# GpSimd's convolved channels: from 32 SBUF-to-SBUF transfers a chunk to 12 by way of device memory, with new orders

## The chip, the cores and the metric

One core of one Trainium2 chip. The metric is the device time of the kernel in microseconds (us). Before the change it is 2811.06 us, the median of 3 runs (2805.05 to 2817.03).

## The reference

The input `x` has 8 sequences of 4096 tokens with 192 channels. Each channel goes through a causal filter of 7 taps; the taps are the softmax of `weight`, one set for each of 8 heads of 24 channels. The result goes through a layer with a rational activation:

```python
h = x @ w_in                                  # [32768, 192] @ [192, 2048]
P = a[0] + a[1]*h + a[2]*h**2 + a[3]*h**3
Q = 1.0 + abs(b[0])*abs(h) + abs(b[1])*h**2
out = (P / (Q + 1e-6)) @ w_out                # [32768, 2048] @ [2048, 192]
```

All inputs and outputs are float32.

## The kernel before, in words

The 32768 tokens are worked in 64 chunks of 512. The 2048 hidden features of a chunk are eight units of 256. For a unit `k` the steps are named by one letter each in the order tables:

- `g1` (`gemm1`, L436): ten matmuls on TensorE, five for each half `a` and `b`, from the convolved tokens into a PSUM tile `hp` of which there are two. The five use the high and low part of the weights (`wh_t`, `wl_t`) and of the tokens: `A` (high part of 128 channels), `L` (its low part) and `B` (high and low part of the other 64 channels). The first matmul of the five already reads `A`, the fourth and fifth read `B`.
- `p`, `A`, `B`, `L`, `Y` on ScalarE (L477, L488, L491, L497, L504), `u` on GpSimd (L481), `v`, `m`, `e`, `g` on VectorE (L485, L508, L512, L516), and `Q`, an accumulating DMA that GpSimd issues (L494). They evaluate P/Q. `v` is the last reader of `hp`.
- `g2` (`gemm2`, L454): the second product, into two PSUM tiles `o0` and `o1`, one for each half of the tokens. `O` (L464, L465) evacuates them and stores the result.

The convolution has two parts. Ninety-six channels are convolved on TensorE for two chunks at a time (`c`, L351), into the same PSUM tiles `o0` and `o1`; ScalarE (`xh`, L375) and VectorE (`xl`, L382) turn this into the high and low part in tile `xh0`, which holds `A` and `L`. These two write all 128 partitions; of every 32 partitions the last 8 are then overwritten. The other 96 channels are convolved on GpSimd (`fir`, steps `f0` to `f8`), which leaves their high and low parts in `fh`, laid out as four token quarters of 32 partitions. `fill` (L411) brings them to the tokens' layout with plain DMAs on SyncE's queue (`move`, L409): sixteen of 32 partitions x 128 tokens into tile `xh1`, which is `B`, and sixteen of 8 partitions x 2 x 128 into the rows of `xh0` that are left. The profile drops the numbers of names, so both tiles read as `xh`. `mv0` is the first sixteen, `mv1` the second; the second sixteen have to come after `xl` of their chunk.

What sets the order: three tables of steps (`START`, `PLAN` once for every two chunks, `END`), which fix the order on TensorE, ScalarE, VectorE and GpSimd. In `g10b.3` the digit behind `g1` is the unit, `b` the half, and the number behind the point says how many chunks back from the newest one. The DMAs on SyncE's queue are not held to the table; they stand in the order that the framework gives them, and each waits there for what it needs, with all behind it waiting too. `POOL_H` and `POOL_L` say for which weight blocks GpSimd makes the high part and the low part at the start; the low parts that GpSimd doesn't make take two matmuls and a copy on VectorE.

Of the kernel before, what the change touches and what calls it, by code (L numbers as in the profile page):

```python
# [50 lines left out]


PLAN = """
g23c.5 g24a.5 g24c.5 g25a.5 v0.4 Y6.5 m6.5 p1.4 e6.5 g6.5 L7.5 A1.4 g12a.4 g12b.4 p2.4 Y7.5 f8.3 mv0.3 u1.4
v1.4 m7.5 Q1.4 e7.5 B2.4 u2.4 g25b.5 g25d.5 g25c.5 g26a.5 g13b.4 g7.5 L0.4 f0.2 A2.4 Q2.4 g13a.4 B3.4 g26b.5
g26d.5 v2.4 Y0.4 p3.4 u3.4 A3.4 L1.4 g26c.5 g27a.5 g27b.5 g27d.5 g27c.5 g14b.4 O0.5 m0.4 e0.4 g0.4 O1.5 Y1.4
g14a.4 B4.4 p4.4 v3.4 c0.3 xh0.3 xh0.2 m1.4 e1.4 f1.2 xl0.3 mv1.3 Q3.4 L2.4 u4.4 g1.4 A4.4 Q4.4 xl0.2 f2.2
v4.4 g15b.4 g15a.4 Y2.4 p5.4 B5.4 u5.4 m2.4 e2.4 f3.2 g2.4 L3.4 g20a.4 g20c.4 g21a.4 g21c.4 ld1.1 A5.4 Q5.4
g16a.4 g16b.4 B6.4 v5.4 g20b.4 g20d.4 Y3.4 g21b.4 g21d.4 p6.4 m3.4 u6.4 A6.4 Q6.4 L4.4 f4.2 f5.2 e3.4 g22a.4
g3.4 v6.4 g17a.4 g17b.4 p7.4 g22b.4 Y4.4 m4.4 e4.4 g4.4 g22c.4 g23a.4 g23c.4 B7.4 L5.4 A7.4 u7.4 v7.4 g10b.3  # L60
g10a.3 g22d.4 g23b.4 g23d.4 g24b.4 B0.3 Y5.4 m5.4 e5.4 Q7.4 g5.4 p0.3 f6.2 L6.4 A0.3 u0.3 v0.3 Q0.3 f7.2
ld0.1 g11a.3 g11b.3 p1.3 Y6.4 m6.4 e6.4 g6.4 g24a.4 B1.3 g24c.4 f8.2 mv1.2 mv0.2 g24d.4 u1.3 g25a.4 A1.3
v1.3 g12b.3 g12a.3 L7.4 Q1.3 g25b.4 p2.3 g25d.4 Y7.4 B2.3 A2.3 m7.4 f0.1 L0.3 u2.3 e7.4 Q2.3 g26b.4 g7.4
g26d.4 v2.3 g13b.3 g13a.3 p3.3 Y0.3 m0.3 B3.3 g25c.4 g26a.4 u3.3 L1.3 e0.3 g0.3 g27b.4 A3.3 v3.3 g27d.4 O1.4
g14b.3 g14a.3 Q3.3 p4.3 Y1.3 f1.1 g26c.4 g27a.4 B4.3 L2.3 u4.3 A4.3 Q4.3 m1.3 g20b.3 e1.3 g1.3 g27c.4 f2.1
O0.4 v4.3 g15a.3 g15b.3 B5.3 g20d.3 g20a.3 Y2.3 m2.3 e2.3 p5.3 g2.3 L3.3 g21b.3 g21d.3 A5.3 u5.3 Q5.3 v5.3
g16a.3 g16b.3 B6.3 g20c.3 g21a.3 Y3.3 m3.3 e3.3 f3.1 p6.3 g3.3 A6.3 u6.3 v6.3 L4.3 g22b.3 g22d.3 g17a.3
g17b.3 p7.3 Y4.3 B7.3 g21c.3 g22a.3 g22c.3 f4.1 m4.3 Q6.3 g23a.3 f5.1 e4.3 A7.3 L5.3 g4.3 g10b.2 u7.3 v7.3
ld1.0 g10a.2 p0.2 Y5.3 g23b.3 g23d.3 m5.3 e5.3 Q7.3 B0.2 f6.1 g24b.3 g24d.3 L6.3 f7.1 g11b.2 u0.2 A0.2
g11a.2 B1.2 Q0.2 g5.3  # L70
"""


START = """
wiw0.0 tp1.0 tp0.0 tp8.0 tp9.0 tp2.0 wiw1.0 tp3.0 tp5.0 wia0.0 tp4.0 wis0.0 wio0.0 wid0.0 wid1.0 wia1.0
wir0.0 wih0.0 wiw2.0 ld0.0 wid2.0 tp6.0 c0.0 wis1.0 cf0.0 wio1.0 cf1.0 wia2.0 wis2.0 wio2.0 wir1.0 cf2.0
wil0.0 wih1.0 wow0.0 woa0.0 wir2.0 wih2.0 wos0.0 xh0.0 wod0.0 xh1.0 xl0.0 wil2.0 wip1.0 woo0.0 wor0.0 wiw3.0
wia3.0 wid3.0 wow1.0 xl1.0 wod1.0 wis3.0 wio3.0 wir3.0 wih3.0 cf3.0 woa1.0 wos1.0 wiw4.0 g10a.0 woo1.0 cf4.0
g10b.0 B0.0 wor1.0 p0.0 u0.0 wia4.0 wil1.0 g11a.0 wid4.0 A0.0 Q0.0 wow2.0 wod2.0 wis4.0 wio4.0 wir4.0 woa2.0
wos2.0 woo2.0 wor2.0 v0.0 g11b.0 A1.0 B1.0 Q1.0 wiw5.0 wia5.0 wis5.0 p1.0 wio5.0 u1.0 wih4.0 wip3.0 wil3.0  # L80
g12a.0 wow3.0 ld1.2 wod3.0 woa3.0 wos3.0 wid5.0 wir5.0 woo3.0 wor3.0 v1.0 wip4.0 wih5.0 wil4.0 L0.0 wiw6.0
wia6.0 wid6.0 Y0.0 g12b.0 B2.0 wis6.0 wio6.0 p2.0 wow4.0 woa4.0 m0.0 wod4.0 e0.0 g13a.0 wir6.0 wos4.0 g13b.0
u2.0 wip5.0 ld0.2 B3.0 A2.0 p3.0 woo4.0 wor4.0 wil5.0 v2.0 wiw7.0 wia7.0 wis7.0 wio7.0 g15a.0 Q2.0 g0.0 u3.0
A3.0 wih6.0 wow5.0 wid7.0 woa5.0 wos5.0 wip6.0 wil6.0 L1.0 woo5.0 wir7.0 wod5.0 wor5.0 Y1.0 v3.0 m1.0 Q3.0
g15b.0 p5.0 e1.0 B5.0 ld0.1 c0.1 xh1.1 xl1.1 xh0.1 xl0.1 L2.0 g14a.0 g14b.0 A4.0 f0.2 g20a.0 g20c.0 g1.0
g21a.0 wow6.0 woa6.0 wos6.0 woo6.0 A5.0 Y2.0 g21c.0 u5.0 v5.0 m2.0 e2.0 g2.0 f1.2 f2.2 wow7.0 g16a.0 woa7.0
wos7.0 woo7.0 g16b.0 B4.0 Q4.0 g22a.0 p4.0 u4.0 v4.0 wih7.0 wil7.0 Q5.0 p6.0 L3.0 B6.0 u6.0 g20b.0 g20d.0
f3.2 f4.2 f5.2 g17a.0 ld1.3 Y3.0 wod7.0 m3.0 e3.0 g3.0 A6.0 g17b.0 p7.0 Q6.0 L4.0 Y4.0 g21b.0 g21d.0 wor7.0
g22b.0 g22d.0 g23b.0 B7.0 u7.0 v6.0 A7.0 Q7.0 L5.0 g10b.1 g10a.1 p0.1 f6.2 f7.2 g22c.0 g23a.0 m4.0 e4.0 g4.0
g23d.0 g24b.0 g24d.0 v7.0 Y5.0 g11a.1 m5.0 B0.1 u0.1 e5.0 g5.0 L6.0 wod6.0 A0.1 Q0.1 g11b.1 wor6.0 B1.1  # L90
"""


END = """
Y6.4 f8.2 mv0.2 g23c.4 v0.3 p1.3 m6.4 g24a.4 g24c.4 u1.3 A1.3 g25a.4 f0.1 L7.4 e6.4 g6.4 g12a.3 g12b.3 Q1.3
v1.3 p2.3 Y7.4 m7.4 e7.4 B2.3 u2.3 g7.4 f1.1 A2.3 v2.3 g25b.4 g25d.4 g26b.4 g26d.4 Q2.3 L0.3 g13b.3 g13a.3
p3.3 Y0.3 m0.3 B3.3 u3.3 g25c.4 g26a.4 L1.3 g26c.4 g27b.4 g27d.4 e0.3 O1.4 g0.3 A3.3 f2.1 v3.3 g27a.4 g27c.4
O0.4 g14b.3 g14a.3 Y1.3 Q3.3 c0.2 p4.3 m1.3 B4.3 u4.3 xh0.2 e1.3 xl0.2 mv1.2 g1.3 g15a.3 L2.3 A4.3 v4.3
xh0.1 xl0.1 Y2.3 m2.3 e2.3 g2.3 f3.1 f4.1 Q4.3 g15b.3 B5.3 p5.3 u5.3 g20a.3 A5.3 g20c.3 f5.1 g21a.3 g21c.3
Q5.3 L3.3 g16a.3 g16b.3 B6.3 v5.3 Y3.3 m3.3 e3.3 g3.3 g20b.3 g20d.3 p6.3 u6.3 A6.3 Q6.3 v6.3 L4.3 g22a.3  # L100
g22c.3 f6.1 f7.1 g17b.3 g17a.3 p7.3 Y4.3 m4.3 e4.3 g4.3 B7.3 g21b.3 g21d.3 g22b.3 g23a.3 A7.3 L5.3 g10a.2
g10b.2 p0.2 g22d.3 u7.3 Y5.3 v7.3 B0.2 m5.3 e5.3 g5.3 g23b.3 Q7.3 L6.3 A0.2 u0.2 v0.2 g11b.2 g11a.2 B1.2
Q0.2 Y6.3 m6.3 e6.3 f8.1 mv0.1 mv1.1 p1.2 g6.3 g23c.3 g24a.3 g24c.3 g25a.3 L7.3 A1.2 g12b.2 u1.2 v1.2 Q1.2
g12a.2 p2.2 Y7.3 B2.2 u2.2 m7.3 e7.3 g7.3 L0.2 A2.2 v2.2 g23d.3 g24b.3 g24d.3 Q2.2 g13b.2 g13a.2 p3.2 g25c.3
g25b.3 g25d.3 g26b.3 Y0.2 g14b.2 m0.2 e0.2 B3.2 u3.2 g0.2 L1.2 A3.2 v3.2 g14a.2 p4.2 Y1.2 m1.2 Q3.2 e1.2
g26d.3 g1.2 B4.2 u4.2 g27b.3 g27d.3 L2.2 g15b.2 A4.2 O1.3 Q4.2 g15a.2 p5.2 v4.2 Y2.2 m2.2 e2.2 B5.2 g26a.3
g26c.3 g27a.3 g27c.3 u5.2 g2.2 L3.2 A5.2 g16b.2 Q5.2 g16a.2 B6.2 v5.2 g20b.2 g20d.2 g21b.2 Y3.2 g21d.2 p6.2
L4.2 m3.2 e3.2 g3.2 A6.2 g17a.2 u6.2 Q6.2 g17b.2 O0.3 B7.2 Y4.2 v6.2 m4.2 e4.2 p7.2 A7.2 g22b.2 g4.2 g22d.2
g20a.2 g20c.2 g10b.1 g10a.1 u7.2 L5.2 g21a.2 v7.2 p0.1 Q7.2 Y5.2 m5.2 e5.2 g23b.2 g23d.2 B0.1 g24b.2 g11a.1
u0.1 A0.1 g11b.1 g21c.2 L6.2 g5.2 g22a.2 g22c.2 p1.1 Y6.2 v0.1 m6.2 e6.2 B1.1 A1.1 g6.2 g23a.2 Q0.1 u1.1  # L110
v1.1 Q1.1 g12a.1 L7.2 g12b.1 p2.1 Y7.2 g23c.2 g24a.2 g24c.2 m7.2 e7.2 g7.2 B2.1 u2.1 A2.1 v2.1 Q2.1 L0.1
g13b.1 g13a.1 p3.1 Y0.1 m0.1 e0.1 g0.1 B3.1 u3.1 A3.1 Q3.1 g25a.2 g25c.2 g24d.2 g25b.2 g14b.1 v3.1 L1.1
g14a.1 B4.1 Y1.1 m1.1 e1.1 g1.1 g26a.2 g26c.2 g27a.2 g27c.2 p4.1 u4.1 O0.2 g15b.1 g15a.1 A4.1 v4.1 g25d.2
g26b.2 g26d.2 L2.1 p5.1 Y2.1 m2.1 Q4.1 e2.1 g2.1 B5.1 u5.1 A5.1 v5.1 Q5.1 g16a.1 L3.1 g16b.1 B6.1 g20a.1
g20c.1 g21a.1 Y3.1 p6.1 m3.1 e3.1 g3.1 g17b.1 g17a.1 A6.1 u6.1 v6.1 g21c.1 g22a.1 g22c.1 L4.1 p7.1 Y4.1 m4.1
e4.1 g4.1 g27b.2 g27d.2 B7.1 O1.2 g23a.1 Q6.1 u7.1 g23c.1 A7.1 v7.1 g20b.1 g20d.1 g21b.1 g21d.1 g22b.1 L5.1
Y5.1 g24a.1 g22d.1 g23b.1 L6.1 Y6.1 g23d.1 g24b.1 m5.1 e5.1 m6.1 g5.1 e6.1 Q7.1 g6.1 L7.1 Y7.1 m7.1 g24d.1
e7.1 g25b.1 g24c.1 g25a.1 g25c.1 g26a.1 g26c.1 g25d.1 g26b.1 g26d.1 g7.1 g27a.1 g27c.1 O0.1 g27b.1 g27d.1
O1.1
"""  # L120


# [519 lines left out]
```

## Time and profile before

| what | value |
|---|---|
| median of 3 runs | 2811.06 us |
| the profiled execution's own time | 2802.48 us |
| its span, first to last instruction | 2800.6 us |
| TensorE matmul busy | 2647.5 us, 95% |
| VectorE busy | 2544.2 us, 91% |
| ScalarE busy | 2528.5 us, 90% |
| GpSimd busy | 2291.8 us, 82% |
| mean busy share of the DMA engines in slices | 0.6 to 0.7 |
| mean granted TensorE clock | 0.978 |

The kernel is periodic: two chunks take about 86 us, and the 64 chunks are 32 such pairs, of which 31 have GpSimd's part (the first pair's tokens are convolved on TensorE alone). A busy TensorE is not TensorE at its peak, since matmuls overlap; what it waits for and how long is read from the idle time ahead of an instruction. A wait is put down to what came last by the profile, so that the same wait can carry different names in different pairs.

### The profile page before, as it was taken

What the parts mean: (1) busy time and instruction counts of PE and PEld (TensorE: products, weight loads), DVE (VectorE), ACT (ScalarE), POOL (GpSimd) and SP (SyncE); (2) the same over time, 40 slices, a digit from 0 to 9 for tenths busy, and PEclk for the clock granted to TensorE, in tenths of its full rate; (3) what the DMA queues carried; (4) which work ended last, traced back from release to release, by engine and by line L of the source; (5) the groups of instructions that cost most, each with busy time, mean ns of one, the idle gap of its engine ahead of it and who ended that gap; (6) DMA issues with size and microseconds to landing.
All of it is one profiled execution on the core that took longest, in us unless ns stands there. A gap on an engine that the chain in (4) does not pass through costs nothing.

```text
span 2800.6 us, 50009 instructions
## 1 busy us (share of the span) xinstructions
PE 2647.5 (95%) x18007; PEld 2381.5 (85%) x18007; DVE 2544.2 (91%) x2185; ACT 2528.5 (90%) x2798; POOL 2291.8 (82%) x1866
## 2 busy tenths in 40 slices
...
GB/s 211 129 148 152 128 148 124 147 154 126 144 134 142 157 137 135 139 133 147 154 127 148 130 142 156 132 141 132 138 152 137 138 137 137 147 153 125 139 122 105
DMA packets 207159, 393.81 MB, mean 141 GB/s; under 512 B 37184, under 2 KB 127808, under 8 KB 206912
## 3 DMA queue, kind: packets, MB, share of 16 engines
...
q8 instruction: 142, 2.33, 0.3%
...
q10 hardware_dynamic: 288, 0.04, 0.0%
...
## 4 chain that ended last, share of the span: by engine, by line
PE 45%; SPq 17%; ACT 13%; issue 9%; POOL 6%; DMA 6%; DVE 5%; POOLq 0%; ACTq 0%; DVEq 0%
PE hp L436 23%; PE o L454 21%; SPq L409 17%; ACT t L477 3%; POOL t L481 3%; ACT B L491 3%; ACT B L497 3%; ACT A L488 2%; DMA out<-ob 2%; DMA xh<-fh 2%; DVE y L512 2%; ACT y L504 1%; POOL prod L400 1%; DMA A<-B 1%; POOL A L494 1%
## 5 line engine op out<-in xcount | busy, mean ns | idle before, releaser
L481 POOL TENSOR_TENSOR t<-t,B 128x1024 f32<-128x1024 f32 x512 | 1255.3, 2452 | 432.6 <-ACT t L477 288.9
L454 PE MATMUL o<-wo_t,t 128*128 128x192 f32 x8192 | 1419.2, 328 | 2.3 <-DVE t L516 1.2
L454 PEld LDWEIGHTS o<-wo_t,t 128*128 128x128 f32 x8192 | 1364.0, 191 | 47.8 <-DVE t L516 2.5
L436 PE MATMUL hp<-xh,wh_t 128*128 128x512 f32 x3072 | 1136.8, 424 | 129.7 <-DMA xh<-fh 84.6
L508 DVE SCALAR_TENSOR_TENSOR t<-t,cf,y 128x1024 f32<-128x1024 f32 x510 | 652.2, 1279 | 197.6 <-ACT y L504 186.6
L436 PE MATMUL hp<-xh,wl_t 128*128 128x512 f32 x2048 | 824.7, 403 | 1.5 <-DVE wl_t L338 1.1
L436 PEld LDWEIGHTS hp<-xh,wh_t 128*128 128x128 f32 x3072 | 596.3, 194 | 267.8 <-DVE t L516 84.7
L491 ACT ACTIVATE B<-hp 128x1024 f32<-128x1024 f32 x512 | 527.3, 1030 | 179.8 <-PE hp L436 175.5
L485 DVE SCALAR_TENSOR_TENSOR t<-hp,cf,t 128x1024 f32<-128x1024 f32 x512 | 654.4, 1278 | 21.7 <-POOL t L481 15.9
L516 DVE SCALAR_TENSOR_TENSOR t<-y,t 128x1024 f32<-128x1024 f32 x510 | 624.2, 1224 | 16.3
L512 DVE SCALAR_TENSOR_TENSOR y<-A,y 128x1024 f32<-128x1024 f32 x510 | 623.5, 1223 | 0.0
L477 ACT ACTIVATE t<-hp 128x1024 f32<-128x1024 f32 x512 | 528.2, 1032 | 48.0 <-PE hp L436 35.5
L497 ACT ACTIVATE B<-A 128x1024 f32<-128x1024 f32 x512 | 550.5, 1075 | 7.6 <-DMA A<-B 7.5
L504 ACT ACTIVATE y<-B 128x1024 f32<-128x1024 f32 x510 | 529.2, 1038 | 10.2 <-DVE t L516 8.5
L488 ACT ACTIVATE A<-hp 128x1024 f32<-128x1024 f32 x512 | 530.9, 1037 | 0.5 <-PE hp L436 0.5
L494 POOL DMA_DIRECT2D A<-B x512 | 474.4, 927 | 29.8 <-ACT A L488 23.5
L436 PEld LDWEIGHTS hp<-xh,wl_t 128*128 128x128 f32 x2048 | 398.7, 195 | 68.6 <-DVE wl_t L338 1.5
L389 POOL TENSOR_SCALAR prod<-xt,tw,zero 128x384 f32<-128x384 f32 x434 | 312.6, 832 | 0.1
L400 POOL TENSOR_TENSOR prod<-prod 128x384 f32<-128x384 f32 x186 | 230.9, 1241 | 3.3 <-DVE t L516 0.8
...
L406 POOL TENSOR_TENSOR fh<-prod,fh 128x384 fp32r<-128x384 f32 x62 | 72.0, 1161 | 2.6
L464 ACT ACTIVATE ob<-o 128x384 f32<-128x384 f32 x128 | 61.2, 508 | 8.2 <-PE o L454 8.2
...
## 6 DMA issues: line engine op xcount, KB each, us to landing
A<-B POOLq DMA_DIRECT2D x512, 512.0 KB, 5.0
...
out<-ob SPq DMA_DIRECT2D x128, 192.0 KB
...
```

What stands on the lines that cost most here:

```text
L436: nc.tensor.matmul(H[k][:, j, :], lhsT=w[:, i, part, j, :], rhs=x, start=(n == 0), stop=(n == len(terms) - 1))
L454: nc.tensor.matmul(op[:, t, 0:D], lhsT=g[:, j * CH + tok:j * CH + tok + P], rhs=wo_t[:, f, :], start=(f == 0 and t == 0), stop=(f == FT - ...
L477: nc.scalar.activation(out=tile_of(k, "t", tpool), in_=flat(k), func=AF.Identity, bias=1.0, scale=scales[2])
L481: nc.gpsimd.tensor_tensor(out=t, in0=t, in1=st[k]["B"], op=ALU.mult)
L485: nc.vector.scalar_tensor_tensor(out=t, in0=flat(k), scalar=k1, in1=t, op0=ALU.mult, op1=ALU.add)
L488: nc.scalar.activation(out=tile_of(k, "A", work), in_=flat(k), func=AF.Abs, scale=scales[0])
L491: nc.scalar.activation(out=tile_of(k, "B", work), in_=flat(k), func=AF.Square, scale=scales[1])
L497: nc.scalar.activation(out=st[k]["B"], in_=st[k]["A"], func=AF.Ln, bias=C_Q)
L504: nc.scalar.activation(out=st[k]["y"], in_=st[k]["B"], func=AF.Exp, scale=-1.0)
L508: nc.vector.scalar_tensor_tensor(out=t, in0=t, scalar=k0, in1=st[k]["y"], op0=ALU.add, op1=ALU.mult)
L512: nc.vector.scalar_tensor_tensor(out=y, in0=st[k]["A"], scalar=C_Q, in1=y, op0=ALU.add, op1=ALU.mult)
L516: nc.vector.scalar_tensor_tensor(out=t, in0=st[k]["y"], scalar=2.0, in1=t, op0=ALU.subtract, op1=ALU.mult)
```

## The change

`fill` has three parts in place of two. Part 0 stores `fh` in a scratch tensor `far` in device memory with four transfers, one for each token quarter; part 1 loads `B` from there with four, part 2 the rows of `xh0` with four. `far` has two buffers. All twelve are on SyncE's queue. Each byte is thus moved twice, stored and then loaded.

```diff
-POOL_H = (1, 2, 3, 5)
-POOL_L = (2, 7)
+POOL_H = (2, 3)
+POOL_L = (1, 2, 6, 7)
...
+    dpool = ctx.enter_context(tc.tile_pool(name="dpool", bufs=2, space=bass.MemoryType.DRAM))
...
     def fill(c, part):
-        src = X[c, "H"]
-        for q in range(NQ):
-            cols = slice(QT * q, QT * q + QT)
-            if part == 0:
-                if q == 0:
-                    X[c, "B"] = xpool.tile([P, CH], F32R, name="xh1")
-                for n in range(4):
-                    s, t = divmod(n, 2)
-                    move(X[c, "B"][BLK * s + t:BLK * s + BLK:2, cols], src[QR * q:QR * q + QR, s, QT * t:QT * t + QT])
-            else:
-                for g in range(NG):
-                    move(X[c, "AL"][32 * g + HD:32 * g + 32, :, cols],
-                         src[QR * q + 8 * g:QR * q + 8 * g + 8, :, 2 * QT:])
+        if part == 0:
+            X[c, "D"] = dpool.tile([QR, 2, NT, CH], F32, name="far")
+            for q in range(NQ):
+                move(X[c, "D"][:, :, :, QT * q:QT * q + QT],
+                     X[c, "H"][QR * q:QR * q + QR].rearrange("p s (t n) -> p s t n", t=NT))
+        elif part == 1:
+            X[c, "B"] = xpool.tile([P, CH], F32R, name="xh1")
+            for n in range(4):
+                s, t = divmod(n, 2)
+                move(X[c, "B"][BLK * s + t:BLK * s + BLK:2], X[c, "D"][:, s, t])
+        else:
+            for g in range(NG):
+                move(X[c, "AL"][32 * g + HD:32 * g + 32], X[c, "D"][8 * g:8 * g + 8, :, 2])
```

The three tables are written anew as a whole. A part of `PLAN` around the convolution of a pair, before and now:

```diff
-g14a.4 B4.4 p4.4 v3.4 c0.3 xh0.3 xh0.2 m1.4 e1.4 f1.2 xl0.3 mv1.3 Q3.4 L2.4 u4.4 g1.4 A4.4 Q4.4 xl0.2 f2.2
+O0.5 Y1.4 m1.4 e1.4 g14a.4 g14b.4 B4.4 Q3.4 c0.3 p4.4 g15b.4 xh0.3 xl0.3 g15a.4 L2.4 A4.4 g20a.4 g20c.4 g1.4
+g21a.4 g21c.4 u4.4 v4.4 xh0.2 xl0.2 Y2.4 g16a.4 m2.4 p5.4 B5.4 e2.4 g20b.4 A5.4 L3.4 f2.2 g16b.4 Q4.4 u5.4
```

What this moves is seen in the order of instructions on three engines. First SyncE's queue over one pair of chunks, before. `8x2x128` are the moves into `xh0`, `32x128` those into `xh1`; the number behind `xh` tells the tiles apart.

```order
L465 DMA out<-ob 128x2x192 x2
L189 DMA xs_107<-in_xa 128x864
L409 DMA xh_3195<-fh 8x2x128 x16
L194 DMA xt<-in_xt 128x402
L409 DMA xh_3421<-fh 32x128
L409 DMA xh_3197<-fh 8x2x128 x16
L409 DMA xh_3421<-fh 32x128 x15
L465 DMA out<-ob 128x2x192 x2
L194 DMA xt<-in_xt 128x402
L409 DMA xh_3756<-fh 32x128 x16
```

The same queue over one pair of chunks in the changed kernel:

```order
L467 DMA out<-ob 128x2x192 x2
L191 DMA xs_110<-in_xa 128x864
L411 DMA xh_5186<-far 8x2x512 x4
L196 DMA xt<-in_xt 128x402
L411 DMA far<-fh 192x1x128 x4
L411 DMA xh_5209<-far 8x2x512 x3
L467 DMA out<-ob 128x2x192
L411 DMA xh_5209<-far 8x2x512
L411 DMA xh_5577<-far 32x512 x3
L467 DMA out<-ob 128x2x192
L411 DMA xh_5577<-far 32x512
L196 DMA xt<-in_xt 128x402
```

Behind the load of `xs` and the convolution there now stand four transfers into `xh0` of the pair's first chunk in place of sixteen. Of its second chunk, four stores come first, then the loads into `xh0` and `xh1`, with two stores of results between them.

Second, VectorE where a pair's convolution is evacuated (L382, now L384), before and now. L485 (now L487) is `v`, which frees an `hp`; L516 (now L518) is `g`.

```order
L382 TENSOR_TENSOR xh_7629<-o_7555,xh_7629 128x512
L516 SCALAR_TENSOR_TENSOR t<-y,t 128x1024
L382 TENSOR_TENSOR xh_7631<-o_7556,xh_7631 128x512
L485 SCALAR_TENSOR_TENSOR t<-hp,cf,t 128x1024
L508 SCALAR_TENSOR_TENSOR t<-t,cf,y 128x1024
```

```order
L384 TENSOR_TENSOR xh_7289<-o_7207,xh_7289 128x512
L518 SCALAR_TENSOR_TENSOR t<-y,t 128x1024
L487 SCALAR_TENSOR_TENSOR t<-hp,cf,t 128x1024
L384 TENSOR_TENSOR xh_7312<-o_7208,xh_7312 128x512
L510 SCALAR_TENSOR_TENSOR t<-t,cf,y 128x1024
```

The first chunk's evacuation stands where it stood; the second chunk's comes one instruction later, behind `v`.

Third, GpSimd where the low part of a pair's second chunk goes into `fh` (L406, now L408), before and now. L481 (now L483) is `u`, one for each unit.

```order
L400 TENSOR_TENSOR prod<-prod 128x384
L481 TENSOR_TENSOR t<-t,B 128x1024
L494 DMA A<-B 128x1024
L403 CAST fh<-prod 128x384
L406 TENSOR_TENSOR fh<-prod,fh 128x384
L481 TENSOR_TENSOR t<-t,B 128x1024
L494 DMA A<-B 128x1024
```

```order
L483 TENSOR_TENSOR t<-t,B 128x1024
L496 DMA A<-B 128x1024
L402 TENSOR_TENSOR prod<-prod 128x384
L405 CAST fh<-prod 128x384
L483 TENSOR_TENSOR t<-t,B 128x1024
L408 TENSOR_TENSOR fh<-prod,fh 128x384
L496 DMA A<-B 128x1024
```

The first `u` of both pieces is that of unit 0 of the chunk then in `gemm1`. The last step of `fh` stood ahead of the `u` of unit 1 and now stands behind it, one unit later.

## Rows read from the trace of the kernel before

**Rows 1.** The page, busy time of each engine.
```profile
PE 2647.5 (95%) x18007; PEld 2381.5 (85%) x18007; DVE 2544.2 (91%) x2185; ACT 2528.5 (90%) x2798; POOL 2291.8 (82%) x1866
```

**Rows 2.** Who waited for whom, whole span: us in total, times, longest us.
```profile
ACT B L491 <- PE hp L436: 175.5, 73, 6.8
...
PE hp L436 <- DMA xh<-fh: 84.6, 24, 4.2
...
PE hp L436 <- DVE t L516: 20.6, 6, 3.6
...
PE hp L436 <- DVE t L485: 12.1, 16, 4.5
PE y L360 <- DVE wb_t L257: 11.0, 1, 11.0
...
PE hp L436 <- DMA xt<-in_xt: 8.5, 2, 4.3
...
ACT B L497 <- DMA A<-B: 7.5, 9, 1.2
```

**Rows 3.** Stretches: us, busy us of PE, PEld, DVE, ACT, POOL, clock, DMA.
```profile
1320.90:1407.00 86.10, 82.17 (x561) 74.32 (x561) 78.46 (x67) 78.33 (x86) 71.89 (x59) 0.98 0.72 142
...
1388.00:1402.00 14.00, 13.84 (x76) 12.59 (x74) 13.31 (x12) 13.56 (x15) 11.71 (x10) 1.00 0.99 197
```

**Rows 4.** The chain of waits, in order of time: start, us, what.
```profile
1387.31 0.66 DVE xh L382
...
1387.98 0.75 SPq L409
...
1403.72 1.86 DMA xh<-fh
...
1405.78 4.11 PE hp L436 x10
...
1409.89 2.60 PE o L454 x16
...
1414.77 2.60 PE o L454 x16
```

**Rows 5.** Timeline of TensorE and VectorE: start, us, instruction [idle before].
```profile
1384.70 1.59 PE L351 MATMUL o<-wb_t,xs 64*32 64x58 f32 x144
...
1399.67 1.27 DVE L485 SCALAR_TENSOR_TENSOR t<-hp,cf,t 128x1024 f32<-128x1024 f32 x1
...
1405.78 0.50 PE L436 MATMUL hp<-xh,wh_t 128*128 128x512 f32 x1 [3.93 <-DMA xh<-fh]
```

**Rows 6.** Timeline of SyncE's queue: start, us, instructions.
```profile
1330.69 28.99 SPq L409 DMA_DIRECT2D xh<-fh  x32
1359.79 1.04 SPq L465 DMA_DIRECT2D out<-ob  x2
...
1386.36 0.35 SPq L189 DMA_DIRECT2D xs<-in_xa  x1
1387.98 16.42 SPq L409 DMA_DIRECT2D xh<-fh  x16
```

**Rows 7.** Timeline of GpSimd.
```profile
1330.75 1.01 POOL L406 TENSOR_TENSOR fh<-prod,fh 128x384 fp32r<-128x384 f32 x1
```

**Rows 8.** Timeline of TensorE, first matmul of the pair's second chunk.
```profile
1360.69 0.53 PE L436 MATMUL hp<-xh,wh_t 128*128 128x512 f32 x1
```

**Rows 9.** The chain of waits: transfers to and from device memory.
```profile
1.23 4.06 DMA ab_t<-in_ab
9.47 5.73 DMA prod<-in_x
...
436.47 2.90 DMA out<-ob
...
1100.77 3.77 DMA out<-ob
```

**Rows 10.** Tile A: its accumulating DMA, from issue to landing.
```profile
DMA to landing us min/median/max: 4.5/5.0/9.0
```

More of the change, by code (lines that the diff above doesn't have):

```diff
@@ L53 @@
 PLAN = """
-g23c.5 g24a.5 g24c.5 g25a.5 v0.4 Y6.5 m6.5 p1.4 e6.5 g6.5 L7.5 A1.4 g12a.4 g12b.4 p2.4 Y7.5 f8.3 mv0.3 u1.4
-v1.4 m7.5 Q1.4 e7.5 B2.4 u2.4 g25b.5 g25d.5 g25c.5 g26a.5 g13b.4 g7.5 L0.4 f0.2 A2.4 Q2.4 g13a.4 B3.4 g26b.5
-g26d.5 v2.4 Y0.4 p3.4 u3.4 A3.4 L1.4 g26c.5 g27a.5 g27b.5 g27d.5 g27c.5 g14b.4 O0.5 m0.4 e0.4 g0.4 O1.5 Y1.4
-g14a.4 B4.4 p4.4 v3.4 c0.3 xh0.3 xh0.2 m1.4 e1.4 f1.2 xl0.3 mv1.3 Q3.4 L2.4 u4.4 g1.4 A4.4 Q4.4 xl0.2 f2.2
-v4.4 g15b.4 g15a.4 Y2.4 p5.4 B5.4 u5.4 m2.4 e2.4 f3.2 g2.4 L3.4 g20a.4 g20c.4 g21a.4 g21c.4 ld1.1 A5.4 Q5.4
@@ L59 @@
[L59 to L68, printed above, removed]
@@ L69 @@
-ld1.0 g10a.2 p0.2 Y5.3 g23b.3 g23d.3 m5.3 e5.3 Q7.3 B0.2 f6.1 g24b.3 g24d.3 L6.3 f7.1 g11b.2 u0.2 A0.2
-g11a.2 B1.2 Q0.2 g5.3
+ld0.1 m5.5 e5.5 ld1.2 g5.5 A0.4 v0.4 L6.5 g23b.5 g23d.5 g24b.5 g24d.5 g11a.4 g11b.4 f6.3 B1.4 Y6.5 g23c.5
+g24a.5 g24c.5 Q0.4 g25a.5 f7.3 m6.5 e6.5 g6.5 p1.4 u1.4 f8.3 mv0.3 A1.4 Q1.4 v1.4 L7.5 g12b.4 g12a.4 p2.4
+Y7.5 B2.4 g25b.5 g25d.5 u2.4 g25c.5 g26a.5 f0.2 A2.4 L0.4 m7.5 e7.5 g7.5 v2.4 g13b.4 g13a.4 B3.4 g26b.5
+g26d.5 Y0.4 m0.4 e0.4 g0.4 Q2.4 p3.4 g27b.5 g27d.5 O1.5 A3.4 u3.4 v3.4 f1.2 mv1.3 g26c.5 g27a.5 L1.4 g27c.5
@@ new lines @@
+O0.5 Y1.4 m1.4 e1.4 g14a.4 g14b.4 B4.4 Q3.4 c0.3 p4.4 g15b.4 xh0.3 xl0.3 g15a.4 L2.4 A4.4 g20a.4 g20c.4 g1.4
+g21a.4 g21c.4 u4.4 v4.4 xh0.2 xl0.2 Y2.4 g16a.4 m2.4 p5.4 B5.4 e2.4 g20b.4 A5.4 L3.4 f2.2 g16b.4 Q4.4 u5.4
+B6.4 g20d.4 g21b.4 g2.4 g22a.4 Q5.4 v5.4 Y3.4 p6.4 u6.4 f3.2 A6.4 Q6.4 L4.4 f4.2 m3.4 e3.4 g3.4 g21d.4 v6.4
+g17b.4 g17a.4 p7.4 Y4.4 B7.4 u7.4 m4.4 g22b.4 A7.4 e4.4 g4.4 ld1.1 g22c.4 f5.2 g23a.4 g23c.4 L5.4 mv2.3
+g10a.3 v7.4 g10b.3 g22d.4 B0.3 Y5.4 g23b.4 g23d.4 m5.4 p0.3 Q7.4 g24b.4 L6.4 e5.4 g5.4 g11a.3 g11b.3 A0.3
@@ new lines @@
+p1.3 u0.3 v0.3 g24a.4 g24c.4 Y6.4 m6.4 g25a.4 B1.3 g24d.4 g12b.3 g12a.3 L7.4 Q0.3 e6.4 g25b.4 g25d.4 f6.2
+f7.2 g6.4 A1.3 u1.3 v1.3 f8.2 g26b.4 p2.3 g26d.4 Q1.3 Y7.4 m7.4 B2.3 u2.3 L0.3 f0.1 g13a.3 e7.4 g13b.3 g7.4
+A2.3 v2.3 p3.3 Q2.3 Y0.3 g25c.4 g26a.4 B3.3 u3.3 L1.3 m0.3 f1.1 e0.3 g0.3 g27b.4 g27d.4 A3.3 Q3.3 O1.4 v3.3
+mv0.2 g14a.3 g14b.3 p4.3 Y1.3 m1.3 e1.3 g1.3 g26c.4 B4.3 u4.3 g27a.4 g27c.4 g20b.3 L2.3 O0.4 g15b.3 A4.3
+v4.3 g15a.3 B5.3 Q4.3 f2.1 Y2.3 m2.3 p5.3 g20a.3 e2.3 g2.3 A5.3 g20d.3 g21b.3 g21d.3 u5.3 g16b.3 v5.3 Q5.3
```

86 lines of the change are left out of this document (45 added, 41 removed).

## The prediction

> **What bounds the kernel now.** I read the busy times first: TensorE's matmuls cover 95% of the span, VectorE and ScalarE 91 and 90%, GpSimd 82% [rows 1]. So time can come only from TensorE's idle time and from stretches in which it runs slowly. Next, who waited for whom [rows 2]. TensorE's first matmul of `gemm1` waited 84.6 us in 24 waits for the DMA `xh<-fh`, 20.6 us in 6 under the name of VectorE's `g`, 8.5 us in 2 under that of the load of `xt`. These 32 waits of some 3.6 us are, but for a small one, one wait with three names. It comes once in each of the 31 pairs of chunks that have GpSimd's part, 86 us apart, and in the timeline the wait is at the first matmul behind the pair's convolution that reads a new chunk: 3.93 us of idle time before 1405.78 [rows 5]. In sum it is 113.7 us.
>
> The chain of waits shows what the matmul waits for [rows 4]. VectorE ends `xl` at 1387.97 (1387.31 + 0.66); at 1387.98 SyncE's queue begins the sixteen moves into `xh0`; the last is issued by 1403.72, lands 1.86 us later, and TensorE starts. The queue's timeline says the same in one row: sixteen moves in 16.42 us, 1.03 us each, right behind the load of `xs` [rows 6]. So the price is one of issuing. The landing is small beside it. TensorE would have been ready at 1405.78 - 3.93 = 1401.85, and VectorE's `v` had freed the `hp` at 1400.94 (1399.67 + 1.27) [rows 5]: without the moves, TensorE would have gone on at once.
>
> The wait costs more than its idle time. The ten matmuls behind it take 4.11 us, where an undisturbed unit has 1414.77 - 1409.89 - 2.60 = 2.28 us for them [rows 4]. The granted clock over this period of 86.1 us is 0.98 [rows 3]; a mean of 0.98 between full speed and half means 3.4 us at the lower of the two levels, 1.2 in place of 2.4 GHz, hence 1.7 us lost per pair. ScalarE's 175.5 us of waits for `hp` in `B` [rows 2] are the echo of the same stall.
>
> One period is thus 86.1 us = 80.7 + 3.7 of idle + 1.7 of low clock. The other engines need 78.46 (VectorE), 78.33 (ScalarE) and 71.89 us (GpSimd) in it [rows 3]. TensorE's 80.7 us is the next limit, with VectorE and ScalarE 2.3 us below it.
>
> **The change part by part.**
>
> *Part 2 of the fill, first chunk of a pair (the wait above).* Behind `xl` stand now four loads in place of sixteen moves; the order rows show the same neighbours, `xs` ahead of them and `xt` behind. No row of before shows a load from `far`. Nearest for the issue are the moves into the same rows at 1.03 us; the stores of results take 0.52 us (two in 1.04) and the load of `xs` 0.35 [rows 6]. For the landing there are two loads from device memory at 4.06 us (small) and 5.73 us (384 KB) [rows 9], and 1.86 us for a move [rows 4]. I take 1.03 and, nearest in kind and size, 4.06: 4 x 1.03 + 4.06 = 8.2 us behind `xl`. The lower end is 4 x 0.35 + 1.86 = 3.3 us, the upper one 4 x 1.81 + 5.73 = 13.0 us, with 1.81 (28.99 us / 16) as if each issue took twice what one of 32 did [rows 6]. TensorE wants the data 1401.85 - 1387.97 = 13.9 us behind `xl`; between the convolution and this matmul the new table has as many halves of `gemm1` and steps of `gemm2` as the old (6 and 13). At all three values the wait is gone. What covers it is 5.7 us of TensorE's own work.
>
> *Parts 0 and 1 and the second chunk.* `fh` of the second chunk was ready at 1331.76 (1330.75 + 1.01) [rows 7], its 32 moves took 28.99 us [rows 6], and its first matmul came at 1360.69 [rows 8]: this chunk had no margin to speak of. Now GpSimd ends `fh` one unit later, (1414.77 - 1409.89 =) 4.88 us [rows 4], at 1336.6. Four stores: 4.1 us. The first load then waits on the queue until they have landed; stores to device memory landed in 2.90 and 3.77 us [rows 9], I take 3.8. Eight loads: 8.2 us; two stores of results between them: 1.0; landing 4.1. Sum 21.2 us, done at 1357.8, 2.9 us ahead of 1360.69, and the last load fills `B`, which only the fourth matmul reads. Cost 0. With 5.73 for the last landing it is still 1.3 us ahead. What waits behind the parked queue is the stores of results and the load of `xt`, neither on TensorE's path in this stretch. For the first chunk stores and loads of `B` stand ahead of the convolution and are done long before.
>
> *GpSimd.* `fh` is one tile; its next CAST waits for four stores in place of 32 moves. Gain 0, GpSimd isn't the limit.
>
> *The evacuation of the convolution* has the second half one instruction later on VectorE, 1.27 us. `gemm2` into that PSUM tile stands behind two halves of `gemm1` and four steps of `gemm2` and one more half, 3 x 1.14 + 4 x 0.65 = 6.0 us behind the convolution's end at 1386.29 [rows 5], by the shares of a unit in rows 4. `xl` of the first half ended 1.7 us behind that end; then `g` and `v` (1.27 each at most) and the second `xl` (0.66) need 3.2, so 4.9 us. Cost 0, with 1.1 us to spare; at worst a wait of under 1 us a pair.
>
> *The start.* GpSimd makes two more low parts and two fewer high parts; two pairs of matmuls and two copies leave TensorE and VectorE, two casts go to ScalarE. I count 0, with half of the start's own wait of 11.0 us [rows 2] either way as bounds.
>
> *What is late next.* With the stall gone ScalarE and VectorE lose the slack that it gave them. TensorE's waits of this kind before are those for `v`: 12.1 us in 16 [rows 2]. I let that double: +12 us.
>
> **Sum** against the profiled execution: 2800.6 - 113.7 - 31 x 1.7 (52.7) + 12 = 2646 us of span, +1.9 around it = 2648. The median of the runs shown lies 8.6 us above that execution, within their spread of 12; I add half of it: **2652 us**, 5.7% below 2811.06.
>
> **A rule against it.** The rows above put a store's landing in device memory at 2.9 to 3.8 us and let it lie beside other work. The Trainium skill, DMA: Bandwidth & Descriptors, section Anatomy of one DMA, has a fixed cost of about 2 us for each transfer, most of it the receipt of the last byte, and says that the wait can be surprisingly long where the target is HBM. The change puts two such costs in a row for each chunk where there was one. By that page alone the sum would stay as it is if they are covered as reckoned above, and come out as in the first rival if not.
>
> **Rivals.**
>
> *The round trip takes the place of the wait.* Store, landing, load and landing for the second chunk last over 24 us in place of 21.2 (1360.69 - 1336.6). For it: the margin is only 2.9 us, and the DMA engines are 0.99 busy in the stretch where the moves ran [rows 3]. Against it: all four landings taken were high ones, and 32 moves got by with 29 us. A new wait of 3.7 us a pair with its 1.7 of low clock gives all back: 2811 us. Chance 0.06.
>
> *VectorE or ScalarE become the limit.* Their work of 78.4 us fits 80.7 with 2.3 us left, but `v` frees `hp` only 0.9 us before TensorE wants it (1401.85 - 1400.94). If the new order loses 1 to 2.5 us a pair to this, without low clock, that is +30 to +75 us: 2680 to 2725. For it: the small margin. Against it: between stalls TensorE ran with next to no idle time at the same margin. Chance 0.18.
>
> *Slower: the scratch's bytes delay the accumulating DMAs.* A pair gains about 0.77 MB stored and loaded again (64 transfers of 8 to 16 KB were 0.77 MB); at the 197 GB/s of the saturated stretch [rows 3] that is 3.9 us of all engines. If it falls on `Q` in both fills of a pair, ScalarE's `L` and with it TensorE wait 2 x (3.9 + 1.7) = 11.2 us, against 5.4 saved: +180 us, 2990. It decides where `Q` lands later than some 8 us; now it lands in 5.0, at most 9.0 [rows 10], and ScalarE waited 7.5 us for it in the whole run [rows 2]. Chance 0.04. The Trainium skill, Trainium Kernel Development and Optimization, section Key Constraints, has DMAs of all queues interleave on the same 16 engines; that 0.99 row agrees, and it is the reason why this rival isn't left out.
>
> **How the numbers follow.** Forecast (TensorE near its own limit) 0.72, then 0.18, 0.06, 0.04. A difference of 0.5%, 14 us, is about what can be told from none. Faster: 0.72 + 0.18 = 0.90, of which I move 0.01 to the same case: 0.89. Same 0.07, slower 0.04. The range goes from no new waits, a start that gains 5.5 and the profiled execution's own level (2800.6 - 113.7 - 52.7 - 5.5 + 1.9 = 2631, less 5 for spread: 2626) up to the second rival's end, 2725; it leaves out some 0.15.
>
> **What would show it.** Right: no wait of `gemm1` on `xh` above 0.5 us in the steady part; the chain of waits without SyncE's moves; a granted clock near 1.0; a period of 81 us; four loads behind `xl` landed within 10 us. Wrong: a wait of TensorE for a DMA from `far`, for VectorE's `v` in each pair, or ScalarE's `L` waiting for `A<-B` by tens of us.

## The result and the profile after

The changed kernel takes 2646.35 us (median of 4 runs, 2644.52 to 2648.07) against 2808.14 us for the kernel before in the same runs: a ratio of 0.942, 95% interval 0.939 to 0.944, or 5.8% less. A second measurement with other runs gave 2647.78 against 2804.47 us, 0.943 (0.941 to 0.945). Forecast were 2652 us and a range of 2626 to 2725.

The page of the changed kernel, busy time of each engine, to be read beside [rows 1]:

```profile
span 2642.8 us, 48315 instructions
...
PE 2596.0 (98%) x18001; PEld 2342.3 (89%) x18001; DVE 2542.2 (96%) x2183; ACT 2536.9 (96%) x2800; POOL 2286.0 (87%) x1866
...
PE 71%; issue 7%; DMA 6%; ACT 5%; DVE 5%; POOL 4%; SPq 0%; ACTq 0%; POOLq 0%; DVEq 0%
```

The last line is the chain of waits by engine. The same line of the kernel before:

```profile
PE 45%; SPq 17%; ACT 13%; issue 9%; POOL 6%; DMA 6%; DVE 5%; POOLq 0%; ACTq 0%; DVEq 0%
```

The span is 157.8 us shorter. TensorE has the same work but for a few matmuls of the start, and its busy time fell by 2647.5 - 2596.0 = 51.5 us, about what the lower clock cost: the mean granted clock rose from 0.978 to 0.998. Its idle time fell from 153.1 to 46.8 us, by 106.3. The two make the whole. In the chain of waits the share of SyncE's queue (`SPq`) fell from 17% to 0%.

Who waited for whom, to be read beside [rows 2] (us in total, times, longest), first all engines, then the DMA queue's own waits:

```profile
ACT B L499 <- DMA A<-B: 24.6, 35, 1.7
ACT B L493 <- PE hp L438: 20.7, 79, 1.7
...
PE hp L438 <- DVE t L487: 10.6, 26, 2.8
```
```profile
SPq L411 <- DMA far<-fh: 136.3, 123, 3.4
```

TensorE's 32 waits for a transfer are gone, and ScalarE's wait for `hp`, 175.5 us before, fell to 20.7. The row that grew most is ScalarE's `L`, which waits 24.6 us in 35 waits for the accumulating DMA `Q`, before 7.5 in 9. The new wait of the scratch, SyncE's queue for its own stores, is 136.3 us in all, some 2.2 us for each of 62 chunks, and TensorE has no wait for what stands behind it.

One period of the changed kernel (columns as in [rows 3]) has the clock at full speed, and TensorE idle for 0.3 us of 81:

```profile
1253.00:1334.00 81.00, 80.66 (x560) 72.82 (x560) 78.16 (x66) 78.22 (x87) 70.90 (x59) 1.00 0.79 159
```

Rows from the timeline of SyncE's queue over one pair, answering to [rows 6]:

```profile
1343.29 4.46 SPq L411 DMA_DIRECT2D far<-fh  x4
1350.58 2.54 SPq L411 DMA_DIRECT2D xh<-far  x3
...
1358.57 0.48 SPq L411 DMA_DIRECT2D xh<-far  x1
...
1394.23 0.35 SPq L191 DMA_DIRECT2D xs<-in_xa  x1
1396.03 3.62 SPq L411 DMA_DIRECT2D xh<-far  x4
```

Behind `xl`, which ends at 1395.99 (1395.30 + 0.69), the four loads are issued in 3.62 us in place of 16.42, and TensorE comes for them at 1409.41 without a wait:

```profile
1395.30 0.69 DVE L384 TENSOR_TENSOR xh<-o,xh 128x512 fp32r<-128x512 f32 x1
```
```profile
1409.41 0.53 PE L438 MATMUL hp<-xh,wh_t 128*128 128x512 f32 x1
```

From the first matmul of the first of these pairs to that of the last, 30 periods, it was 114.94 to 2699.34 before and is 112.36 to 2542.84 now: 86.15 and 81.02 us a period. That is 153.9 of the 157.8 us; 2.6 came ahead of it, 1.3 behind.

### The profile page after: what moved, and what is told of

It reads as the page before. It is cut to its first block, busy times and chain, and to the rows that moved or that the text cites. A ratio compares the mean times of both kernels' runs of the same rounds, so it can differ in the third digit from the quotient of the medians.

```text
span 2642.8 us, 48315 instructions
## 1 busy us (share of the span) xinstructions
PE 2596.0 (98%) x18001; PEld 2342.3 (89%) x18001; DVE 2542.2 (96%) x2183; ACT 2536.9 (96%) x2800; POOL 2286.0 (87%) x1866
## 4 chain that ended last, share of the span: by engine, by line
PE 71%; issue 7%; DMA 6%; ACT 5%; DVE 5%; POOL 4%; SPq 0%; ACTq 0%; POOLq 0%; DVEq 0%
PE o L456 37%; PE hp L438 33%; DMA A<-B 6%; DVE y L514 2%; POOL t L483 2%; ACT y L506 2%; DVE t L487 1%; ACT t L479 1%; PE o L353 1%; ACT B L493 1%; ACT B L499 1%; DVE t L518 1%; POOL prod L391 1%; POOL A L496 1%; ACT A L490 0%
## 5 line engine op out<-in xcount | busy, mean ns | idle before, releaser
L483 POOL TENSOR_TENSOR t<-t,B 128x1024 f32<-128x1024 f32 x512 | 1253.8, 2449 | 312.4 <-ACT t L479 154.5
L438 PE MATMUL hp<-xh,wh_t 128*128 128x512 f32 x3072 | 1109.0, 415 | 13.8 <-DVE t L487 10.6
L438 PE MATMUL hp<-xh,wl_t 128*128 128x512 f32 x2048 | 802.8, 392 | 0.0
L438 PEld LDWEIGHTS hp<-xh,wh_t 128*128 128x128 f32 x3072 | 579.1, 189 | 138.9 <-DVE t L487 20.0
L487 DVE SCALAR_TENSOR_TENSOR t<-hp,cf,t 128x1024 f32<-128x1024 f32 x512 | 653.9, 1277 | 17.9 <-POOL t L483 10.8
L518 DVE SCALAR_TENSOR_TENSOR t<-y,t 128x1024 f32<-128x1024 f32 x510 | 624.1, 1224 | 16.4
L499 ACT ACTIVATE B<-A 128x1024 f32<-128x1024 f32 x512 | 547.2, 1069 | 24.9 <-DMA A<-B 24.6
L493 ACT ACTIVATE B<-hp 128x1024 f32<-128x1024 f32 x512 | 524.5, 1024 | 24.5 <-PE hp L438 20.7
L438 PEld LDWEIGHTS hp<-xh,wl_t 128*128 128x128 f32 x2048 | 386.6, 189 | 64.1 <-issue 1.4
L391 POOL TENSOR_SCALAR prod<-xt,tw,zero 128x384 f32<-128x384 f32 x434 | 302.6, 763 | 0.1
L402 POOL TENSOR_TENSOR prod<-prod 128x384 f32<-128x384 f32 x186 | 214.3, 1152 | 1.3 <-DMA prod<-prod 1.0
L398 POOL DMA_DIRECT2D prod<-prod x62 | 70.3, 1134 | 1.5 <-issue 1.2
L353 PEld LDWEIGHTS o<-wb_t,xs 64*32 64x32 f32 x4464 | 46.7, 105 | 19.6 <-issue 19.3
```

Source lines behind the costliest of these rows:

```text
L438: nc.tensor.matmul(H[k][:, j, :], lhsT=w[:, i, part, j, :], rhs=x, start=(n == 0), stop=(n == len(terms) - 1))
L483: nc.gpsimd.tensor_tensor(out=t, in0=t, in1=st[k]["B"], op=ALU.mult)
L487: nc.vector.scalar_tensor_tensor(out=t, in0=flat(k), scalar=k1, in1=t, op0=ALU.mult, op1=ALU.add)
L493: nc.scalar.activation(out=tile_of(k, "B", work), in_=flat(k), func=AF.Square, scale=scales[1])
L499: nc.scalar.activation(out=st[k]["B"], in_=st[k]["A"], func=AF.Ln, bias=C_Q)
L518: nc.vector.scalar_tensor_tensor(out=t, in0=st[k]["y"], scalar=2.0, in1=t, op0=ALU.subtract, op1=ALU.mult)
```

## The experiments

The theory: TensorE waited for the sixteen transfers behind `xl`, because each takes the queue about 1 us; fewer transfers end the wait and with it the lower clock. The rivals: the new orders did it; or the moves from SBUF to SBUF were slow as such. A last group asks what limits the kernel now.

**The scratch alone, with the old orders.** The kernel before with `far` and the new `fill` (stores ahead of whichever part comes first), all tables as they were.

```diff
+        if (c, "D") not in X:
+            X[c, "D"] = dpool.tile([QR, 2, NT, CH], F32, name="far")
...
         if part == 0:
...
-                    move(X[c, "B"][BLK * s + t:BLK * s + BLK:2, cols], src[QR * q:QR * q + QR, s, QT * t:QT * t + QT])
+                move(X[c, "B"][BLK * s + t:BLK * s + BLK:2], X[c, "D"][:, s, t])
```

> The kernel before with the scratch alone: the three tables and the weight blocks stay as they were, only the 32 moves become 4 stores and 8 loads. Theory (the transfers behind xl are what TensorE waited for, the orders hardly matter): the wait of 3.6 us a pair and its low clock of 1.7 us are gone, the period falls from 86.1 to about 81 us, time 2640 to 2670 us. Rival (the new orders bring the gain or half of it): a wait of 1.5 us or more a pair stays, the period is 83 us or more, time 2700 us or more.

Measured: 2625.23 us, ratio 0.935 (0.933 to 0.938). The theory holds, and the scratch alone does more than the whole change: its period is (2520.77 - 111.36) / 30 = 80.31 us, from the first matmul of the first of the pairs to that of the last. ScalarE's wait for `Q` stays as it was before the change:

```profile
ACT B L498 <- DMA A<-B: 7.7, 13, 1.1
```

Since this sets the new orders in a poor light, it was run again, to be set against both measurements of the changed kernel.

> The old tables with the scratch once more, to set it against the changed kernel's two measurements (2646 and 2648 us). Theory (the new orders lose some 20 us that the scratch alone has): 2618 to 2630 us. Rival (the two differ by chip and not by order): 2636 to 2650 us.

Measured: 2625.16 us, ratio 0.936 (0.934 to 0.937), with the changed kernel at 0.943 (0.941 to 0.945). The intervals don't meet: the old orders with the scratch are the faster ones, by about 21 us.

**The new orders alone, with the 32 moves of before.**

```diff
-            if part == 0:
+            if part == 1:
...
-            else:
+            elif part == 2:
```

> The changed kernel's tables with the 32 moves of before, out of SBUF. Theory: the sixteen moves behind xl come back at about 1 us each, 16.4 + 1.9 - 13.8 = 4.5 us of wait a pair and 1.7 us of low clock, 2646 + 31 x 6.2 = 2840 us; between 2790 and 2950, since the second chunk's 32 moves take 29 us and its GpSimd part now ends one unit later, which may add a second wait of up to 5 us a pair. Rival (the orders bring the gain): below 2730 us.

Measured: 3006.99 us, ratio 1.071 (1.068 to 1.074). The orders bring nothing without the scratch. TensorE now waits in both chunks of a pair. Two such rows, the first a pair's first chunk, the second its second one (timeline of TensorE):

```profile
116.67 0.47 PE L437 MATMUL hp<-xh,wh_t 128*128 128x512 f32 x1 [3.85 <-DMA xh<-fh]
...
162.22 0.77 PE L437 MATMUL hp<-xh,wh_t 128*128 128x512 f32 x1 [3.77 <-DMA xh<-fh]
```

Its span of 3005.0 us is 362 us above the changed kernel's, 11.7 us a pair: two waits of 3.8 and two stretches at a lower clock (its mean is 0.945). The time lies outside the 2790 to 2950 that were written down: the second wait, put there as one that may come, came in each pair, and with a stretch at a lower clock of its own, for which the estimate had no term.

**Sixteen loads out of device memory.** The changed kernel, with the first chunk's part 2 cut into quarters:

```diff
-                move(X[c, "AL"][32 * g + HD:32 * g + 32], X[c, "D"][8 * g:8 * g + 8, :, 2])
+                n = 128 if c % 2 == 0 else CH
+                for at in range(0, CH, n):
+                    move(X[c, "AL"][32 * g + HD:32 * g + 32, :, at:at + n], X[c, "D"][8 * g:8 * g + 8, :, 2, at:at + n])
```

> The changed kernel, but for the first chunk of each pair the four loads behind xl are cut to sixteen of a quarter each, same bytes, still from device memory. Theory (the count of transfers on the one queue is the price, not where the data comes from): sixteen issues of 0.8 to 1.0 us and a landing of 2 to 4 us against 13.8 us of cover, so 1 to 6 us of wait a pair, and 1.7 us of low clock where it is over 3 us: 2680 to 2890 us, with TensorE waiting for the DMA from far in nearly each pair. Rival (what cost time was the move from SBUF to SBUF itself): no wait, 2646 us.

Measured: 2824.08 us (one run). The timelines of SyncE's queue and of TensorE in this run:

```profile
1316.90 16.39 SPq L411 DMA_DIRECT2D xh<-far  x16
```
```profile
1335.56 0.72 PE L440 MATMUL hp<-xh,wh_t 128*128 128x512 f32 x1 [3.99 <-DMA xh<-far]
```

Sixteen loads from device memory take 16.39 us, sixteen moves from SBUF took 16.42 [rows 6]. The wait is back with all its cost, though the bytes, their source and the orders are those of the fast kernel. It is the number of transfers, not where they read. The cut also makes four times as many pieces, each a quarter as long, but the price doesn't follow the pieces: a store into `far` has 192 of 128 values, a load here 16, and four stores took 4.46 us, 1.11 each.

**Eight loads.** As before, with halves (256 in place of 128).

> As the run with sixteen loads, but the first chunk's four loads behind xl are cut to eight halves. Theory: eight issues of 0.8 to 1.0 us and a landing of 2 to 4 us are 8.4 to 12 us against a cover of 13.8 us, so no wait: 2640 to 2655 us. Rival (any further transfer behind xl costs its 1 us at once): 31 x 4 = 124 us more, 2770 us.

Measured: 2639.29 us (one run). Its eight loads are issued in 8.95 us, and no wait of `gemm1` on `xh` shows. So the cover of 13 to 14 us is real: four more transfers under it cost nothing, twelve more bring the wait back.

**The wait filled with other matmuls.** The kernel before, with 14 matmuls that have no use ahead of the one that waits:

```diff
+        if c >= NS and c % 2 == 0 and i == 0 and j == 1:
+            for n in range(14):
+                nc.tensor.matmul(H[k][:, j, :], lhsT=wh_t[:, 0, 0, 0, :], rhs=X[c - 1, "A"], start=True, stop=True)
```

> The kernel before with 14 matmuls added ahead of the first matmul of gemm1 that waits in each pair; they read a chunk that is there, write into the free hp, and are overwritten. They take about 14 x 0.228 = 3.2 us, inside the wait of 3.6 us. Theory (1.7 us a pair are lost to the lower clock behind the wait, apart from the wait itself): the wait's place is filled, the ten matmuls behind it take 2.3 instead of 4.1 us, 31 x 1.7 = 53 us less: 2755 us, 2745 to 2775. Rival (the clock behind the wait costs nothing, since what follows would wait anyway): 2800 to 2815 us.

Measured: 2764.12 us, ratio 0.985 (0.982 to 0.988). More work, 46 us less time. TensorE's timeline (each row a start, its time, what ran):

```profile
1297.71 3.48 PE L437 MATMUL hp<-xh,wh_t 128*128 128x512 f32 x14
1301.93 0.47 PE L439 MATMUL hp<-xh,wh_t 128*128 128x512 f32 x1 [0.74 <-DMA xh<-fh]
...
1304.30 2.76 PE L457 MATMUL o<-wo_t,t 128*128 128x192 f32 x16
```

The ten matmuls behind the wait take 1304.30 - 1301.93 = 2.37 us, where they took 4.11 [rows 4]. The mean clock is 0.998 in place of 0.978. So the lower clock behind a wait of 3.6 us costs 1.5 to 1.7 us, on top of the wait.

**One step of the new orders moved back.** In the changed kernel ScalarE waits for `Q` just ahead of the first chunk of most pairs. GpSimd's and ScalarE's timelines show why:

```profile
1315.78 0.85 POOL L398 DMA_DIRECT2D prod<-prod  x1
1316.36 1.16 POOL L496 DMA_DIRECT2D A<-B  x1
```
```profile
1326.29 1.06 ACT L499 ACTIVATE B<-A 128x1024 f32<-128x1024 f32 x1 [1.37 <-DMA A<-B]
```

GpSimd issues the filter's own accumulating DMA (576 KB) and `Q` of unit 4 directly behind it. `L`, which needs this `Q`, can start only 9.9 us after its issue (1326.29 - 1316.36), where `Q` at the median has landed after 5.2:

```profile
DMA to landing us min/median/max: 4.5/5.2/10.1
```

In the old table the two stand the other way round. The edit swaps them in `PLAN`:

```diff
-A5.4 L3.4 f2.2 g16b.4 Q4.4 u5.4
+A5.4 L3.4 Q4.4 g16b.4 f2.2 u5.4
```

> The changed kernel with one step moved in PLAN: the accumulating DMA of the filter (f2, 576 KB) of the pair's second chunk is issued behind Q of unit 4 instead of ahead of it. Theory (the new orders lose 0.7 us a pair to the run with the old ones, because this Q lands behind the larger transfer and ScalarE's L of unit 4, VectorE and at last TensorE wait for it): ScalarE's waits for A<-B fall from 24.6 to about 8 us, the period from 81.07 to 80.4 us, time 2622 to 2632 us. Rival (the new orders lose it elsewhere, as in the convolution's evacuation or at the start): 2640 to 2650 us.

> The changed kernel itself once more, on the same chip as the run with the moved step. Both theories: 2640 to 2652 us.

Measured: 2633.78 us with the swap, ratio 0.938 (0.937 to 0.940), and 2647.78 us without it, 0.943 (0.941 to 0.945). Waits of the run with the swap:

```profile
ACT B L499 <- DMA A<-B: 6.6, 17, 1.1
```

The wait fell from 24.6 to 6.6 us and the time by 14 us, some two thirds of the 21 us that the new orders lose to the old ones. The period comes down to (2531.61 - 113.40) / 30 = 80.61 us and not quite to 80.31. What makes up the rest isn't explained; no run took it apart.

**What limits the kernel now.** Four kernels on the old orders with the scratch, each with work left out and each run once; the nine runs of that kernel with all its work lie between 2622.66 and 2627.23 us. First 16 matmuls a pair of TensorE are left out:

```diff
+        if j == 1 and c >= NS:
+            terms = terms[:4]
```

> The old tables with the scratch, and for all chunks but the first two the fifth matmul of gemm1 left out in half b (the low part of the weights times B), 16 matmuls of 0.228 us or 3.65 us of TensorE in each pair. Theory (with the wait gone, TensorE at 80.4 us a pair is the limit and VectorE and ScalarE at 78.4 stand right behind it): the period falls only to about 78.5 to 79.5 us, 31 x 1 to 1.9 = 30 to 60 us less, 2565 to 2595 us. Rival A (TensorE alone is the limit): 31 x 3.65 = 113 us less, 2512 us. Rival B (VectorE or ScalarE are the limit already): 2615 to 2625 us.

Measured: 2642.53 us, 17 us more than with all matmuls. No theory had this. TensorE waits more for VectorE, and ScalarE for `Q`:

```profile
PEld hp L439 <- DVE t L488: 59.0, 141, 3.1
PEld o L457 <- DVE t L519: 54.8, 151, 1.4
ACT B L500 <- DMA A<-B: 33.5, 32, 2.3
```

The chain of waits by engine, first of the scratch with the old orders and all matmuls, then of this run:

```profile
PE 83%; ACT 5%; issue 4%; POOL 3%; DVE 3%; DMA 2%; SPq 0%; ACTq 0%; POOLq 0%; DVEq 0%
```
```profile
issue 25%; DVE 24%; POOL 19%; ACT 18%; PE 6%; DMA 6%; SPq 0%; POOLq 0%; ACTq 0%; DVEq 0%
```

With all matmuls the chain runs through TensorE. An estimate of its bare work: 16 units at 4.88 us and the convolution at 1.59 [rows 4, 5] are 79.7 of the 80.31 us of a period, so it is full. With 3.65 us less the chain hardly touches it, and no single engine has taken its place.

Then VectorE, which leaves out step `e` of one unit in eight:

```diff
     def step_e(k):
         y = st[k]["y"]
+        if k >= NS * UPC and k % UPC == 3:
+            return
```

> The old tables with the scratch, and for all chunks but the first two step e of unit 3 left out, 1.22 us of VectorE a chunk, 2.4 us a pair; TensorE has all its work. Theory (in the run with the old tables TensorE is full, its blocks follow each other without a gap): 2612 to 2628 us, no change. Rival (VectorE sets the period): 31 x 2.4 = 75 us less, 2550 us.

Measured: 2624.70 us, no change: while TensorE has all its work, VectorE's doesn't set the time. Then both cuts together:

> Both cuts: the fifth matmul of half b of gemm1 (3.65 us of TensorE a pair) and step e of unit 3 (2.4 us of VectorE a pair). Theory (TensorE and VectorE stand level, so that cutting TensorE alone brought nothing): the period falls by 1 to 2 us, 2560 to 2600 us. Rival (ScalarE with its waits for the accumulating DMAs, or these DMAs themselves, hold the period where it is): 2615 to 2645 us.

Measured: 2640.24 us. With TensorE and VectorE both relieved the time stays at that of the run with TensorE's cut, so VectorE's work wasn't what held that one. VectorE's `v` now waits for GpSimd's `u`, 80.4 us where it was 12.0 in the run with TensorE's cut alone (that run's row first):

```profile
DVE t L488 <- POOL t L484: 12.0, 41, 1.5
```
```profile
DVE t L488 <- POOL t L484: 80.4, 134, 1.5
```

And with step `L` of the same unit left out too, which takes work from ScalarE:

```diff
     def step_L(k):
+        if k >= NS * UPC and k % UPC == 3:
+            return
```

> The run with both cuts, and step L of unit 3 left out too for all chunks but the first two: 0.93 us of ScalarE a chunk, 1.9 us a pair. Theory (with TensorE cut, ScalarE holds the period): 31 x 1.9 = 58 us less than 2640 us: 2575 to 2605 us. Rival (the accumulating DMAs or GpSimd hold it): 2625 to 2645 us.

Measured: 2617.33 us, 23 us less, where 58 were expected if ScalarE alone held the period and none if it didn't. It settles only this much: step `L`, ScalarE's work or its wait for `Q` there, has a part in it. ScalarE's waits for `Q` moved to another instruction and stayed as long (a wait row of this run: `A` waits instead of `L`):

```profile
ACT A L491 <- DMA A<-B: 30.6, 27, 2.0
```

The orders were written for TensorE's full work; with less, each engine keeps its fixed order and meets the others at other moments. What exactly holds the period once TensorE has less to do stays open; no run took work from GpSimd.

## Why the prediction was right, point by point

The sum was made of two large terms, and both can be read off the page. *Low clock*, 52.7 us: TensorE's busy time fell by 51.5 us, and filling the wait alone brought 46. *Idle time*, 113.7 us less 12 of new waits, so 101.7: it fell by 106.3. The period was forecast at 81 us and is 81.02. The span came out at 2642.8 where 2646 was reckoned.

That it came so close is in part luck. The two terms alone would leave a span of 2634 us; the scratch with the old orders, which has no loss by new orders, has 2621.0:

```profile
span 2621.0 us, 48261 instructions
...
PE 2586.1 (99%) x18007; PEld 2342.6 (89%) x18007; DVE 2540.3 (97%) x2185; ACT 2533.9 (97%) x2798; POOL 2292.9 (87%) x1866
```

There TensorE's busy time fell by 61.4 us at the same mean clock (0.998) and its idle time by 118.2, so the stall had cost 13 us more than the sum says; where these come from no run shows. The new orders then lost 2642.8 - 2621.0 = 21.8 us, for which the sum has the 12 of new waits. The two misses cancel but for 3 us.

*Part 2 of the fill.* Right in mechanism and margin. Forecast were 8.2 us behind `xl` against 13.9 us of cover; the four loads were issued in 3.62 us (0.91 each, 1.03 was taken), and the cover is 1409.41 - 1395.99 = 13.4 us. The landing wasn't measured; in the run with sixteen loads it was at most 1335.56 - 1333.29 = 2.3 us, and 4.06 was taken. That run shows that the price per transfer was right for this stretch.

*"The price is one of issuing"*: so it is, but the 1.03 us are a mean of unlike issues. Two of the sixteen in the chain of waits of the kernel before, and the shortest, median and longest issue of all its moves (ns, from the view of tile `fh`):

```profile
1390.14 0.69 SPq L409
...
1393.86 1.63 SPq L409
```
```profile
L409 SPq DMA_DIRECT2D xh<-fh x1984: 463/685/2287, 76.3 to 2729.8; - x199
```

At the median of 0.685 sixteen moves would take 11.0 us, with the landing 12.9, and fit the cover of 13.9: the wait came from the number together with issues that were drawn out. In this stretch the DMA engines' share is 0.99 [rows 3]; that this is what draws the issues out isn't shown, as no run kept the sixteen and took the other traffic away.

*The second chunk's round trip*, 21.2 us forecast against 24.1 available, of which 17.1 came ahead of the last landing. These took 15.8 us, from the first store's start to the last load's issue (1343.29 to 1359.05), and 25.3 were there to the matmul:

```profile
1368.56 0.53 PE L438 MATMUL hp<-xh,wh_t 128*128 128x512 f32 x1
```

The stores' landing held the queue for 1350.58 - 1347.75 = 2.8 us where 3.8 was taken. The first rival needed over 24 us and was far off. Of the page's rule (the Trainium skill, DMA: Bandwidth & Descriptors, Anatomy of one DMA) that a wait for a write to HBM can be surprisingly long: that section is on DMAs that GpSimd issues, and these go by SyncE's queue. The 2.8 us are near its fixed cost of about 2, the longest such wait of the run is 3.4, and what there is lies beside other work.

*The evacuation's later half, GpSimd's tile, the start*, each counted at 0: TensorE has no wait for `xl` of over 0.5 us in the steady part, and the start gained 2.6 us with the first wait's 3.29 gone from it, so it lost 0.7 us itself (1.0 against the run with the old orders, whose first period begins at 111.36).

*What is late next*: both the size and the cause were wrong. The prediction took TensorE's waits for `v` and doubled them, +12 us. Those of its matmuls didn't grow (12.1 us before, 10.6 after); those of its weight loads, which lie beside matmuls, did, before and now:

```profile
PEld hp L436 <- DVE t L485: 12.6, 19, 3.2
```
```profile
PEld hp L438 <- DVE t L487: 20.0, 54, 1.0
```

What came instead is a loss of the new orders themselves, 21 us against the old ones with the same scratch, of which the swap of one DMA ahead of another gives 14 back. The tables show it: `Q` of unit 4 stands behind the larger transfer in the new one. The prediction compared GpSimd's order at another place only, though both lines of `PLAN` stand in the section on the change. The third rival had the right victim, `L` waiting for `Q`, and named the scratch's bytes as the cause; with the old orders the same bytes leave that wait at 7.7 us.

*The next limit.* That TensorE is the next limit holds for the run with the old orders, though at 80.31 us and not at 80.7: TensorE is full, and less of VectorE's work changes nothing. "VectorE and ScalarE 2.3 us below it" doesn't say how far the period could fall: with 3.65 us less of TensorE's work the time rose, and with less of VectorE's as well it stayed there.

The changed kernel isn't the best of those run: the scratch with the old orders takes 2625 us and beats both.
